# Inputs laid out in the order of their transfers, in a gated-attention kernel with a two-layer network behind it

## The chip, the cores and the metric

The kernel runs on one core of one Trainium2 chip. The metric is device time of one execution in microseconds. The core's engines are PE (TensorE, matrix products), DVE (VectorE), ACT (ScalarE), POOL (GpSimd) and SP (SyncE, which here only issues transfers); each works through its own instructions in order and waits for others by semaphores. Sixteen DMA engines carry the transfers.

## What is computed

A recurrence over 768 steps for each of 4 x 8 heads with 48 columns, and a two-layer network on its output, 3072 tokens of 384 columns with 2048 hidden ones:

```python
for t in range(S):
    state = alpha[:, :, t, :, None] * state + np.einsum('bhd,bhe->bhde', k[:, :, t], v[:, :, t])
    y[:, :, t] = np.einsum('bhd,bhde->bhe', q[:, :, t], state)
...
h = x @ w_in
beta = 1.0
neg = h <= -beta
pos = h >= beta
...
g = np.where(pos, h, np.where(neg, 0.0, (h + beta) ** 2 / (4.0 * beta)))
...
return (g @ w_out).astype(np.float32)
```

q, k, v and alpha are 32-bit floats; the two weights are 64-bit floats.

## The kernel before, in words

**Chunks.** The 3072 tokens are 24 chunks of 128; three chunks are a group. For each chunk the kernel brings alpha, k and q (`raw_a`, `raw_k`, `raw_q`) to a form with two heads of 64 rows on the partitions and tokens along the free axis. DVE runs a scan over alpha forwards and one backwards (L634, L660), multiplies k into the backward one (`inv`, L674) and q into the forward one (`Q`, L680). PE turns the keys (L701), makes scores (L716), the update of the state (L729) and the outputs (L856). V is used in two places: `vt`, with tokens on the partitions, and `both`, which holds V's rows beside the state, with the halves of the chunk swapped (its second place).

**How the inputs come.** Chunks up to `EARLY` (nine of them) come as they lie in memory, tokens on partitions, 48 columns of 4 bytes a head, which is runs of 192 bytes (L510), into two halves of one tile per input. PE turns each with four transposes (L544) into PSUM, where DVE reads them. Later chunks come by four transfers each (L528) and DVE transposes 32x32 blocks (L557) into `turn`. V's second place is copied from `vt` by ACT or POOL for the first six chunks (L594, L598), and comes by four transfers after that (L605).

**Weights.** Eight pairs of raw weights (L462, L472, L482) come as 64-bit words. ACT (L374, L382, L427), DVE (L390, L401) and POOL (L414, L429, or DVE in their place) decode each half into a high and a low 32-bit part; that is about 2 instructions on DVE, 4 on POOL and 3 on ACT for each of the sixteen halves.

**The network.** A hidden row f of a group is nine products of 128x384 (L952); then DVE and ACT apply the gate (L981, L996, L1007), ACT rounds the result to a high part (L1011), POOL subtracts it for a low part (L1012), and nine more products add into the outputs (L1030). The first `SPLIT` hidden rows of group 0 are done chunk by chunk, in products of 128x128. Groups 0 and 1 do the first half of the hidden rows each, then the second half of each, so that weights are asked for later; the other groups go one by one. Group 0 takes its last rows by way of `rest_b`; for later groups six transfers move the remainder of x into place (L901).

**What sets the order.** A planner, `Plan.order`, places every instruction with a cost in microseconds and a due time, engine by engine. Instructions may have a second engine to go to (`other`). Where it sees PE idle in the first 165 us it puts in fillers, products of zeros (L1101). Of the chunks from `MERGE` on, the outputs of one are merged with the scores of the next in one burst.

Of the kernel before, what the change touches and what calls it, by code (L numbers as in the profile page):

```python
# [8 lines left out]
F32 = mybir.dt.float32  # L9
# [19 lines left out]
EARLY = 9  # L29
# [4 lines left out]
LOAD = 6.0  # L34
# [7 lines left out]
AHEAD = 15.0  # L42
# [3 lines left out]
MERGE = 6  # L46
# [4 lines left out]
VHELP = 6  # L51
SPLIT = 1
# [25 lines left out]
class Plan:  # L78
# [7 lines left out]
    SMALL = 2.1  # L86
# [148 lines left out]
def gated_attention_ffn(ctx: ExitStack, tc: tile.TileContext, q, k, v, alpha, w_in, w_out, out):  # L235
    nc = tc.nc
    B, H, S, D = q.shape
    DM, DF = w_in.shape
    P = 128
    G = H // 2  # L240
# [31 lines left out]
    both = const.tile([P, 2, 2, G, 2, 64], F32, name="both")  # L272
# [47 lines left out]
    with ExitStack() as main:  # L320
# [7 lines left out]
        for name in ("stage", "tp", "qk", "vp", "att", "fw"):  # L328
            pool(name)
# [22 lines left out]
        wide = w_in.dtype == U64  # L352

        def decode(u, which, raw, parts, shape, key):
# [4 lines left out]
            flat = lambda t: t.rearrange(shape)  # L359
            part = lambda a: parts().rearrange(PARTS[which])[:, a * n : (a + 1) * n]  # L360
            w = raw
            data = lambda: flat(raw())
            if wide:
                w = buf("stage", "w", [P, n], 2)
                word = lambda dt, i: flat(raw()).bitcast(dt).rearrange("p (m w) -> p m w", w=2)[:, :, i]
# [47 lines left out]
                for c in cols:  # L413
                    add = lambda e, c=c: e.tensor_tensor(  # L414
                        out=bits()[:, c], in0=bits()[:, c], in1=word(I32, 0)[:, c], op=ALU.add
                    )
                    plan.op(
                        "POOL",
                        0.93,
                        key,  # L420
                        lambda add=add: add(nc.gpsimd),
                        [w, raw, (u, which)],
                        [w],
                        port=True,
                        other=("DVE", 0.9, lambda add=add: add(nc.vector), True),
                    )
            plan.op("ACT", 0.8, key, lambda: nc.scalar.copy(out=part(0), in_=data()), [w], [parts])  # L427
            for c in cols:
# [5 lines left out]
                    0.93,  # L434
# [5 lines left out]
                    other=("DVE", 0.48, lambda sub=sub: sub(nc.vector), True),  # L440
# [4 lines left out]
        def weights(u):  # L445
            fs = slice(u * NW * P, (u + 1) * NW * P)
            make = lambda shape, dt: Buf("wt", lambda: wts.tile(shape, dt, name="wt"))
            ti = make([P, KT, NW * P], w_in.dtype)
            to = make([P, NW, DM], w_out.dtype)
            key = need[u]  # L450
            pairs_of = w_in[0 : 2 * D * KT, fs].rearrange("(k r e) f -> r e k f", r=2, e=D)
            rest = w_in[2 * D * KT : DM, fs].rearrange("(r k e) f -> r e k f", r=2, k=KT)
# [3 lines left out]
            for r in range(2):  # L456
                p = 64 * r
                plan.op(
                    "SP",
                    Plan.ISSUE,  # L460
                    fetch,
                    lambda p=p, r=r: nc.sync.dma_start(out=ti()[p : p + D], in_=pairs_of[r]),  # L462
                    [],
                    [ti],
                    moved=size * 3 // 8,
                    beside=r > 0,
                )
                plan.op(
                    "SP",
                    Plan.ISSUE,  # L470
                    fetch,
                    lambda p=p, r=r: nc.sync.dma_start(out=ti()[p + D : p + 64], in_=rest[r]),  # L472
                    [],
                    [ti],
                    moved=size // 8,
                    beside=True,
                )
# [3 lines left out]
                fetch,  # L481
                lambda: nc.sync.dma_start(out=to(), in_=w_out[fs, :].rearrange("(j p) m -> p j m", p=P)),  # L482
                [],
                [to],
                moved=size,
            )
            wi[u] = make([P, 2, KT, NW, P], F32R)
            wo[u] = make([P, 2, NW, DM], F32R)
            decode(u, "i", ti, wi[u], "p k f -> p (k f)", ready)
            decode(u, "o", to, wo[u], "p j m -> p (j m)", ready + LAG)  # L490


        C = CH // 32
        flat = lambda t: t.rearrange("p g t -> p (g t)")
        pairs = lambda t: t[:, 0 : G * CH].rearrange("p (g t) -> p g t", g=G)

        def whole(t, j):

            half = t.rearrange("p g w -> p (g w)")[:, j % 2 * H * 64 : (j % 2 + 1) * H * 64]
            return half.rearrange("p (h e) -> p h e", e=64)  # L500

        def load(x, j, key):
            b, t0 = j // PER, j % PER * CH
            t, rows = raws[x], {"a": alpha, "k": k, "q": q}[x][b, :, t0 : t0 + CH, :]
            if j < EARLY:
                plan.op(
                    "SP",
                    Plan.ISSUE,
                    key,
                    lambda: nc.sync.dma_start(out=whole(t, j)[:, :, 0:D], in_=rows.rearrange("h s d -> s h d")),  # L510
                    [],
                    [(x, j % 2)],
                    moved=P * DM * 4 * Plan.SMALL,
                )
                return
            if j == EARLY:
                plan.op(
                    "POOL", 0.15, key, lambda: nc.gpsimd.memset(t[:, :, W : W + 32], 1.0), [], [(x, 0), (x, 1)]
                )
            view = rows.rearrange("(g r) (a c) d -> r a g (c d)", r=2, c=C)  # L520
            for r in range(2):
                for half in range(2):
                    p0, o = 64 * r + 32 * half, 32 * (1 - half)
                    plan.op(
                        "SP",
                        Plan.ISSUE,
                        key,
                        lambda p0=p0, o=o, r=r: nc.sync.dma_start(out=t[p0 : p0 + 32, :, o : o + W], in_=view[r]),  # L528
                        [],
                        [(x, 0), (x, 1)],  # L530
                        moved=P * DM * 2,
                        beside=r + half > 0,
                    )

        def turned(x, j, key, to=()):

            t = raws[x]
            if j < EARLY:
# [3 lines left out]
                def flip():  # L542
                    for g in range(G):
                        nc.tensor.transpose(  # L544
                            out=view()[:, g * CH : (g + 1) * CH],
                            in_=whole(t, j).rearrange("p h e -> p (h e)")[:, g * P : (g + 1) * P],
# [3 lines left out]
                flips[j] = plan.op("PE", 0.45, key, flip, [(x, j % 2)], [ps, *to], mode="full", after=[flips[j]] if j in flips else [])  # L550
                return ps, view
            o = buf("tp", "turn", [P, G * CH], 2)
            plan.op(
                "DVE",
                1.05,
                key,
                lambda: nc.vector.transpose(  # L557
                    out=pairs(o()).rearrange("p g (a c) -> p g c a", c=C),
                    in_=t[:, :, 32 : 32 + W].rearrange("p g (c d) -> p g c d", d=D)[:, :, :, 0:32],
                ),  # L560
                [(x, 0), (x, 1)],
                [o],
            )
            return o, lambda: o()
# [3 lines left out]
        def prepare(j, key):  # L568

            b, t0 = j // PER, j % PER * CH  # L570
            early = j < EARLY
            for x in "akq":
# [6 lines left out]
                lambda: nc.sync.dma_start(out=vt(), in_=v[b, :, t0 : t0 + CH, :].rearrange("h s d -> s h d")),  # L579
                [],  # L580
                [vt],
                moved=P * DM * 4 * Plan.SMALL,
            )
            for r in range(2):
                rows = slice(HC * (1 - r), HC * (2 - r))
                for u in range(2):
                    if j < VHELP:
                        to = both[rows, j % 2, u, :, r, 0:D]
                        from_ = lambda r=r, u=u: vt()[HC * u : HC * (u + 1)].rearrange("p (g r) d -> r p g d", r=2)[r]
                        plan.op(  # L590
                            "ACT",
                            0.36,
                            key + 0.2,
                            lambda to=to, from_=from_: nc.scalar.copy(out=to, in_=from_()),  # L594
                            [vt],
                            [("v", j % 2, u)],
                            beside=r > 0,
                            other=("POOL", 0.38, lambda to=to, from_=from_: nc.gpsimd.tensor_copy(out=to, in_=from_()), True),  # L598
                        )
                        continue  # L600
                    plan.op(
                        "SP",
                        Plan.ISSUE,
                        key - LOAD + 1,
                        lambda r=r, u=u, rows=rows: nc.sync.dma_start(  # L605
                            out=both[rows, j % 2, u, :, r, 0:D],
# [561 lines left out]
def stepwise(tc, q, k, v, alpha, win, wout, NF, ident, half_b, ones, out):  # L1168
# [8 lines left out]
    with ExitStack() as ctx:  # L1177
# [39 lines left out]
        with tc.For_i(0, B * S, P) as r:  # L1217
# [74 lines left out]
```

## Time and profile before

| | us |
|---|---|
| median of the runs | 534.03 |
| lowest, highest | 532.78, 534.27 |
| the profiled execution's own time | 532.99 |
| its span | 531.2 |
| busy: PE, DVE, ACT, POOL | 509.1, 378.7, 264.4, 271.7 |
| PE's wide products, hidden and output (L952, L1030) | 227.0 and 227.8 |

The span is what the profile's rows cover; the execution's own time is 1.8 us longer. Busy PE time contains the fillers. Slices are fortieths of the span, 13.28 us each. In rows of engines, "SPq" is SP's queue of transfer instructions, "PEld" is PE's loading of weights; a row of the waits reads: who waited, for whom, us in total, times, longest.

### The profile page before, as it was taken

The page shows a single profiled execution, that of the slowest core. Times are in us where ns is not written, and L with a number is a line of the kernel's source. Part 1 is how long each engine was busy: PE and PEld are TensorE (multiplying, and loading weights), DVE is VectorE, ACT ScalarE, POOL GpSimd, SP SyncE. Part 2 cuts the span into 40 slices and gives each one's busy share as a digit, 9 for nine tenths or more (in the row PEclk, how much of TensorE's full clock was granted, in tenths as well). Part 3 has the DMA queues.
Part 4 walks back from the last instruction along what each step waited for, and adds up shares of the span by engine and source line. Part 5 has one row for each costly group of instructions (what it writes and reads, how often), then busy time and mean ns, then how long its engine had stood idle before and what let it go on. Part 6 is the DMA issues. An engine that isn't in the chain of part 4 may idle for free.

```text
span 531.2 us, 12704 instructions
## 1 busy us (share of the span) xinstructions
PE 509.1 (96%) x4906; PEld 488.4 (92%) x4906; DVE 378.7 (71%) x714; ACT 264.4 (50%) x510; POOL 271.7 (51%) x332
## 2 busy tenths in 40 slices
PE   8896999798999999999999999999999999999995
PEld 6785899698899999999999999999999999999994
DVE  6998778577899796688696796688596884333331
ACT  3789897565444443444444433434434534343332
POOL 4687888699854452443452452453443452333330
PEclk9999799999999999999999999999999999999998
DMA  9999889921455634335334442345333200100001
GB/s 160 194 216 203 179 197 170 255 50 47 109 145 140 181 76 91 91 82 136 90 73 90 131 111 56 91 83 135 90 85 84 74 23 2 23 12 33 2 0 49
DMA packets 112241, 53.87 MB, mean 101 GB/s; under 512 B 77392, under 2 KB 107056, under 8 KB 112176
## 3 DMA queue, kind: packets, MB, share of 16 engines
q1 hardware_dynamic: 112176, 53.01, 44.4%
q8 instruction: 40, 0.66, 0.5%
q14 instruction: 25, 0.20, 0.1%
HBM read 45.02 MB, written 5.90 MB: 96 GB/s over the span
## 4 chain that ended last, share of the span: by engine, by line
PE 77%; DMA 5%; POOL 5%; ACT 4%; SPq 3%; DVE 3%; issue 2%; POOLq 0%; DVEq 0%; ACTq 0%
PE ps L1030 34%; PE ps L952 33%; DMA wt<-in_moe_w_in 5%; PE ps L856 4%; PE ps L729 2%; POOL wt L429 2%; PE ps L716 2%; POOL w L414 2%; PE ps L701 2%; POOL gh L1012 1%; ACT w L374 1%; SPq L510 1%; SPq L462 1%; DVE Q L634 1%; PE ps L544 1%
## 5 line engine op out<-in xcount | busy, mean ns | idle before, releaser
L1030 PE MATMUL ps<-wt,gh 128*128 128x384 f32 x1152 | 227.8, 341 | 4.4 <-POOL gh L1012 2.5
L952 PE MATMUL ps<-ring,wt 128*128 128x384 f32 (+1 forms) x1170 | 227.0, 339 | 1.9 <-DVE gf L1007 1.1
L1012 POOL TENSOR_TENSOR gh<-gf,gh 128x384 fp32r<-128x384 f32 (+1 forms) x129 | 139.7, 1084 | 166.0 <-ACT gh L1011 134.9
L952 PEld LDWEIGHTS ps<-ring,wt 128*128 128x128 f32 x1170 | 206.2, 190 | 3.8 <-DVE gf L1007 1.4
L1030 PEld LDWEIGHTS ps<-wt,gh 128*128 128x128 f32 x1152 | 200.5, 188 | 8.0 <-POOL gh L1012 4.1
L981 ACT ACTIVATE gf<-gf,half_b 128x384 f32<-128x384 f32 x122 | 74.9, 616 | 113.2 <-DVE gf L996 110.0
L1011 ACT CAST gh<-gf 128x384 fp32r<-128x384 f32 (+1 forms) x130 | 65.9, 507 | 85.9 <-DVE gf L1007 64.6
L996 DVE TENSOR_SCALAR gf<-ps 128x384 f32<-128x384 f32 x122 | 67.2, 552 | 56.5 <-PE ps L952 54.2
L1007 DVE TENSOR_TENSOR gf<-gf,ps 128x384 f32<-128x384 f32 (+1 forms) x130 | 69.8, 539 | 47.7 <-ACT gf L981 47.6
L414 POOL TENSOR_TENSOR w<-w,wt 128x384 int32<-128x384 int32 x31 | 32.7, 1070 | 10.4 <-DVE w L401 3.9
L429 POOL TENSOR_TENSOR wt<-w,wt 128x384 fp32r<-128x384 f32 x32 | 35.2, 1114 | 1.4 <-ACT wt L427 0.9
L856 PE MATMUL ps<-Q,both 128*64 128x64 f32 x372 | 27.8, 229 | 2.6 <-DVE inv L660 2.6
L856 PEld LDWEIGHTS ps<-Q,both 128*64 128x64 f32 x372 | 24.4, 141 | 5.2 <-issue 3.8
L856 PE MATMUL ps<-other,both 128*64 128x64 f32 x372 | 27.7, 229 | 0.3 <-POOL other L784 0.3
L802 DVE TENSOR_TENSOR Q<-ps,mask 64x256 f32<-64x256 f32 x48 | 20.3, 423 | 7.9 <-ACT other L766 5.2
L833 POOL TENSOR_TENSOR state<-state,last 128x192 f32<-128x192 f32 x20 | 10.1, 507 | 30.0 <-DVE state L758 29.9
L634 DVE TENSOR_TENSOR_SCAN Q<-turn,fwd 128x512 f32<-128x512 f32 x15 | 20.5, 1365 | 6.6 <-PE ps L856 6.5
L856 PEld LDWEIGHTS ps<-other,both 128*64 128x64 f32 x372 | 24.3, 141 | 0.4 <-POOL other L784 0.4
L748 ACT COPY both<-state 48x192 f32<-48x192 f32 x53 | 18.5, 349 | 7.9 <-POOL state L833 4.8
L643 POOL TENSOR_SCALAR last<-Q 128x4 f32<-128x4 f32 x24 | 5.4, 224 | 31.4 <-DVE Q L634 30.8
L680 POOL TENSOR_TENSOR Q<-Q,turn 128x512 f32<-128x512 f32 x15 | 19.5, 1299 | 3.4 <-DVE turn L557 3.4
L401 DVE SCALAR_TENSOR_TENSOR w<-wt,w 128x768 int32<-128x768 int32 x16 | 20.6, 1285 | 0.2
(92 smaller groups left out, 511.5 us busy)
## 6 DMA issues: line engine op xcount, KB each, us to landing
wt<-in_moe_w_out SPq DMA_DIRECT2D x8, 768.0 KB, 7.9
raw_a<-in_alpha SPq DMA_DIRECT2D x60, 96.0 KB, 2.2
raw_k<-in_k SPq DMA_DIRECT2D x60, 96.0 KB, 2.4
raw_q<-in_q SPq DMA_DIRECT2D x60, 96.0 KB, 2.4
vt<-in_v SPq DMA_DIRECT2D x24, 192.0 KB, 3.3
wt<-in_moe_w_in SPq DMA_DIRECT2D x16, 288.0 KB, 5.9
out<-ot SPq DMA_DIRECT2D x24, 192.0 KB, 2.9
both<-in_v SPq DMA_DIRECT2D x72, 48.0 KB, 2.5
```

The source lines that it names most:

```text
L401: lambda: nc.vector.scalar_tensor_tensor(out=bits(), in0=word(I32, 1), scalar=-0x80000000, in1=bits(), op0=ALU.bitwise_and, op1=ALU.bitwis ...
L414: add = lambda e, c=c: e.tensor_tensor(out=bits()[:, c], in0=bits()[:, c], in1=word(I32, 0)[:, c], op=ALU.add)
L429: sub = lambda e, c=c: e.tensor_tensor(out=part(1)[:, c], in0=data()[:, c], in1=part(0).bitcast(F32)[:, c], op=ALU.subtract)
L634: lambda: nc.vector.tensor_tensor_scan(flat(Q()), aT(), flat(fwd), 0.0, ALU.mult, ALU.max),
L856: nc.tensor.matmul(out=ps()[halves[r], to, halves[u]], lhsT=lhsT[:, u, r], rhs=x()[:, g, halves[u]], start=m + u == 0, stop=True, skip_gro ...
L952: nc.tensor.matmul(out=h(), lhsT=win(f, w)[:, kt], rhs=ring[:, at, kt, a, :], start=(m == 0), stop=(m == 3 * KT - 1),)
L981: lambda: nc.scalar.activation(out=gf(), in_=in_(), func=func, scale=scale, bias=bias),
L996: lambda: nc.vector.tensor_scalar(out=gf(), in0=h(), scalar1=-1.0, scalar2=1.0, op0=ALU.max, op1=ALU.min),
L1007: lambda: nc.vector.tensor_tensor(out=gf(), in0=gf(), in1=h(), op=ALU.max),
L1011: plan.op("ACT", 0.08 + 0.41 * w, key + 0.4, lambda: nc.scalar.copy(out=gh()[:, 0], in_=gf()), [gf], [gh])
L1012: sub = lambda e: e.tensor_tensor(out=gh()[:, 1], in0=gf(), in1=gh()[:, 0].bitcast(F32), op=ALU.subtract)
L1030: nc.tensor.matmul(out=o_ps[seg][t](), lhsT=gh()[:, a, (t - c0) * CH : (t - c0 + 1) * CH], rhs=wout(f, w), start=(f == f0 and i == 0), sto ...
```

## The change

The host lays every input out with numpy, without arithmetic, as one transfer will fetch it (`lay`): `tok_a`, `tok_k`, `tok_q` with tokens on the partitions and each head padded from 48 to 64 columns with its first columns again; `dim_a`, `dim_k`, `dim_q` already in the turned form, 512 tokens-by-heads wide; V for `vt` and, apart, for `both`; the weights as rows of 768 64-bit words. Each becomes one transfer of 128 partitions (two for `both`), with runs of 1.5 to 6 KB. Every chunk's raw inputs get a buffer of their own, eight in all.

Chunks 0 to 3 are still turned by PE; from the fifth on the `dim_` form is read by DVE from SBUF as it lands, so that neither PE's transposes of chunks 4 to 8 nor DVE's of later ones are there. The product of q (L592 now) has POOL as its first engine from chunk 4 on, where it had DVE up to chunk 8. V's second place comes by transfer for all chunks. The zero columns that the padding needed are no longer set by POOL. Hidden rows 0 and 1 of group 0 are split by chunk, not row 0 alone; merged bursts begin two chunks later; inputs are due 3 us ahead, not 6.

```diff
-EARLY = 9
+EARLY = 4
...
-LOAD = 6.0
+LOAD = 3.0
...
-AHEAD = 15.0
+AHEAD = 12.0
...
-MERGE = 6
+MERGE = 8
...
-SPLIT = 1
+SPLIT = 2
...
-    both = const.tile([P, 2, 2, G, 2, 64], F32, name="both")
+    both = const.tile([P, 2, 2, 2, G, 64], F32, name="both")
...
-            for r in range(2):
-                p = 64 * r
+            for x, t in (("w_in", ti), ("w_out", to)):
                 plan.op(
                     "SP",
                     Plan.ISSUE,
                     fetch,
-                    lambda p=p, r=r: nc.sync.dma_start(out=ti()[p : p + D], in_=pairs_of[r]),
+                    lambda x=x, t=t: nc.sync.dma_start(out=t(), in_=laid[x][u]),
                     [],
-                    [ti],
-                    moved=size * 3 // 8,
-                    beside=r > 0,
-                )
...
+        def load(x, j, key):
+
+            raw = raws[x, j] = buf("stage", "raw", [P, G * CH], 8)
             plan.op(
                 "SP",
                 Plan.ISSUE,
-                fetch,
-                lambda: nc.sync.dma_start(out=to(), in_=w_out[fs, :].rearrange("(j p) m -> p j m", p=P)),
+                key,
+                lambda: nc.sync.dma_start(out=raw(), in_=laid[("tok_" if j < EARLY else "dim_") + x][j]),
                 [],
...
-            o = buf("tp", "turn", [P, G * CH], 2)
-            plan.op(
-                "DVE",
-                1.05,
-                key,
-                lambda: nc.vector.transpose(
-                    out=pairs(o()).rearrange("p g (a c) -> p g c a", c=C),
-                    in_=t[:, :, 32 : 32 + W].rearrange("p g (c d) -> p g c d", d=D)[:, :, :, 0:32],
-                ),
-                [(x, 0), (x, 1)],
-                [o],
-            )
-            return o, lambda: o()
+            return raw, lambda: raw()
...
+                plan.op(
+                    "SP",
+                    Plan.ISSUE,
+                    key - LOAD + 1,
+                    lambda r=r, rows=rows: nc.sync.dma_start(
+                        out=both[rows, j % 2, r].rearrange("p u g e -> p (u g e)"), in_=laid["v_both"][j, rows]
+                    ),
+                    [],
+                    [("v", j % 2, u) for u in range(2)],
+                    moved=P * DM * 4 * 2 // 3,
+                    beside=r > 0,
+                )
...
+    e = np.arange(64) % D
+    for name, x in (("q", q), ("k", k), ("a", alpha)):
+        x = x.reshape(B, H, S // CH, CH, D)[..., e]
+        laid["tok_" + name] = x.transpose(0, 2, 3, 1, 4).reshape(NCH, CH, H * 64)
+        x = x.reshape(B, G, 2, S // CH, CH, 64)
+        laid["dim_" + name] = x.transpose(0, 3, 2, 5, 1, 4).reshape(NCH, P, G * CH)
```

Since the planner sets the order anew, three places are shown as they stand in the two programs. First SP's queue at the start of the program. Before, from the second chunk's inputs on (`raw_`, `vt`: inputs; `wt`: weights):

```order
L510 DMA raw_a<-in_alpha 128x8x48
L510 DMA raw_k<-in_k 128x8x48
L510 DMA raw_q<-in_q 128x8x48
L579 DMA vt<-in_v 128x8x48
L462 DMA wt<-in_moe_w_in 48x3x256
L472 DMA wt<-in_moe_w_in 16x3x256
L462 DMA wt<-in_moe_w_in 48x3x256
L472 DMA wt<-in_moe_w_in 16x3x256
L482 DMA wt<-in_moe_w_out 128x2x384
```

After, from the first chunk's inputs on:

```order
L470 DMA raw<-in_laid_tok_a 128x512
L470 DMA raw<-in_laid_tok_k 128x512
L470 DMA raw<-in_laid_tok_q 128x512
L507 DMA vt<-in_laid_v 128x384
L518 DMA both<-in_laid_v_both 64x512 x2
L447 DMA wt<-in_laid_w_in 128x768
L447 DMA wt<-in_laid_w_out 128x768
L470 DMA raw<-in_laid_tok_a 128x512
```

The first pair of weights has moved ahead of the second chunk's inputs, and V's second place stands ahead of both.

Second, PE at the sixth chunk (chunk 5), from the turning of its keys on. Before (L544 turns inputs, L701 keys; L952 and L1030 are the network):

```order
L544 MATMUL ps<-ident,raw_q 128x128 x4
L701 MATMUL ps<-ident,inv 128x128 x4
L952 MATMUL ps<-ring,wt 128x384 x9
L716 MATMUL ps<-Q,inv 64x64 x16
L1030 MATMUL ps<-wt,gh 128x384 x9
L729 MATMUL ps<-vt,ks 64x48 x8
L952 MATMUL ps<-ring,wt 128x384 x9
L544 MATMUL ps<-ident,raw_a 128x128 x4
L544 MATMUL ps<-ident,raw_k 128x128 x4
```

After (L613 turns keys, L864 and L942 are the network); 25 fillers and nine L942 follow:

```order
L613 MATMUL ps<-ident,inv 128x128 x4
L628 MATMUL ps<-Q,inv 64x64 x16
L942 MATMUL ps<-wt,gh 128x384 x3
L864 MATMUL ps<-ring,wt 128x384 x9
L641 MATMUL ps<-vt,ks 64x48 x8
L864 MATMUL ps<-ring,wt 128x384 x9
```

The transposes of inputs are gone; counted up to chunk 5's outputs, the network has 54 narrow and 36 wide hidden products and 27 output products in place of 27, 36 and 18. In the whole program fillers go from 90 to 128, and L544's 108 transposes become 48 (L485).

Third, POOL at the same chunk. Before (L414 and L429 decode weights, L1012 is the network's subtraction):

```order
L414 TENSOR_TENSOR w<-w,wt 128x384 x3
L784 AFFINE_SELECT other<-other 64x512
L414 TENSOR_TENSOR w<-w,wt 128x384
L643 TENSOR_SCALAR last<-Q 128x4
L429 TENSOR_TENSOR wt<-w,wt 128x384 x3
L833 TENSOR_TENSOR state<-state,last 128x192
L429 TENSOR_TENSOR wt<-w,wt 128x384
L1012 TENSOR_TENSOR gh<-gf,gh 128x384
```

After (L404 and L419 decode, L924 subtracts, L592 is the product of q):

```order
L745 TENSOR_TENSOR state<-state,last 128x192
L654 MEMSET both 48x4x48 x2
L555 TENSOR_SCALAR last<-Q 128x4
L592 TENSOR_TENSOR Q<-Q,raw 128x512
L419 TENSOR_TENSOR wt<-w,wt 128x384
L924 TENSOR_TENSOR gh<-gf,gh 128x128
L924 TENSOR_TENSOR gh<-gf,gh 128x384
L404 TENSOR_TENSOR w<-w,wt 128x384 x4
```

The product of q now stands in POOL's order among the decodes.

More of the change, by code (lines that the diff above doesn't have):

```diff
@@ L424, in decode @@
                         port=True,
-                        other=("DVE", 0.9, lambda add=add: add(nc.vector), True),
+                        other=("DVE", 0.2 + 1.4 / PIECES, lambda add=add: add(nc.vector), True),
                     )
@@ L439, in decode @@
                     port=True,
-                    other=("DVE", 0.48, lambda sub=sub: sub(nc.vector), True),
+                    other=("DVE", 0.08 + 0.8 / PIECES, lambda sub=sub: sub(nc.vector), True),
                 )
@@ L445, in weights @@
         def weights(u):
[L446 removed]
             make = lambda shape, dt: Buf("wt", lambda: wts.tile(shape, dt, name="wt"))
[L448 to L449 removed]
+            ti, to = (make(list(laid[x].shape[1:]), laid[x].dtype) for x in ("w_in", "w_out"))
             key = need[u]
[L451 to L452 removed]
             size = P * NW * DM * (8 if wide else 4)
@@ L494, in gated_attention_ffn @@
[L494 to L508, printed above, removed]
-                    key,
[L510 to L513, printed above, removed]
-                )
[L515 to L529, printed above, removed]
-                        [(x, 0), (x, 1)],
-                        moved=P * DM * 2,
-                        beside=r + half > 0,
-                    )
@@ L585, in prepare @@
                 rows = slice(HC * (1 - r), HC * (2 - r))
[L586 to L606, printed above, removed]
-                            in_=v[b, :, t0 + HC * u : t0 + HC * (u + 1), :].rearrange("(g r) s d -> r s g d", r=2)[r],
-                        ),
-                        [],
-                        [("v", j % 2, u)],
-                        moved=P * DM * Plan.SMALL,
-                        beside=r > 0,
-                    )
+                plan.op(
[10 more added lines that the diff above has]
+                )
             Q, inv = (buf("qk", x, [P, G, CH], 2) for x in ("Q", "inv"))
@@ L848, in outputs @@
             n, i = group_of[j], j % 2
-            parts = [(both[:, i, :, g], g, g) for g in range(KT if n == 0 else G)]
+            parts = [(both[:, i, :, :, g], g, g) for g in range(KT if n == 0 else G)]
             parts += [(rest_b[:, :, :, kt], KT, kt) for kt in range(KT) if n == 0]
```

118 lines of the change are left out of this document (62 added, 56 removed).

## The prediction

> **What bounds the kernel now.** I read the slices of the span first, then busy time by stretch, the chain that ended last, the waits, and the groups by shape. In the slices PE is short of work only at the front, and the wire is full until the eighth slice:
>
> ```profile
> PE   8896999798999999999999999999999999999995
> PEclk9999799999999999999999999999999999999998
> DMA  9999889921455634335334442345333200100001
> GB/s 160 194 216 203 179 197 170 255 50 47 109 145 140 181 76 91 91 82 136 90 73 90 131 111 56 91 83 135 90 85 84 74 23 2 23 12 33 2 0 49
> ```
>
> The same by stretch (busy us and instructions of PE, weight load, DVE, ACT, POOL; then clock, wire share, GB/s):
>
> ```profile
> 0.00:60.00 60.00, 50.82 (x775) 43.34 (x776) 50.56 (x101) 44.94 (x94) 42.05 (x79) 0.95 1.06 194
> 60.00:97.00 37.00, 37.00 (x342) 35.56 (x342) 27.76 (x46) 30.26 (x54) 29.41 (x32) 1.00 0.91 189
> 97.00:108.00 11.00, 7.48 (x32) 6.52 (x31) 7.54 (x14) 5.33 (x10) 8.33 (x9) 0.85 0.94 230
> 108.00:150.00 42.00, 39.29 (x392) 36.89 (x392) 32.98 (x56) 25.14 (x45) 37.76 (x39) 1.00 0.31 82
> 150.00:450.00 300.00, 299.61 (x2945) 291.89 (x2944) 232.76 (x450) 130.47 (x259) 131.83 (x155) 1.00 0.38 92
> 525.00:531.20 6.20, 0.00 (x0) 0.00 (x0) 0.00 (x0) 0.44 (x1) 0.00 (x0) 0.73 0.29 102
> ```
>
> From 150 us on PE is busy 299.61 of 300 us, so what the change takes off DVE there (a 32x32 transpose for each of three inputs of fifteen chunks) is worth nothing. The last 6.20 us are the last rows' way out and the branch, and stay. **Only the first 150 us can become shorter.** There, 0 to 60 is a stretch of DVE (50.56 us busy) with an over-full wire beside it; from 97 to 108 PE lacks 3.5 us; from 108 to 150 it lacks 2.7 with POOL at 37.76 of 42. PE's busy time at the front also holds fillers, and its clock is halved for a while:
>
> ```profile
> L1101 PE MATMUL ps<-zeros 128*128 128x256 bf16 x90 | 12.9, 297 | 1.1 <-DVE zeros L249 1.1
> 54.00:56.00 2.00, 1.90 (x32) 1.82 (x32) 1.90 (x5) 1.46 (x2) 2.00 (x3) 0.50 1.13 301
> ```
>
> **The wire.** From 2 to 8 us only the 192-byte rows of heads move; from 100 to 102 us mostly rows of weights:
>
> ```profile
> DMA packets 5863, 1.11 MB, mean 185 GB/s; under 512 B 5863, under 2 KB 5863, under 8 KB 5863
> DMA packets 372, 0.77 MB, mean 385 GB/s; under 512 B 29, under 2 KB 214, under 8 KB 372
> ```
>
> Packets of 190 B get 185 GB/s, packets of 2.1 KB get 385. After the change every input row is 1.5 to 6 KB long. An early chunk grows from 0.79 MB (four tensors) to 1.25 MB (three padded to 64 columns a head, V, and V's second place), but its wire time goes from 0.79 / 0.185 = 4.3 us to 1.25 / 0.385 = 3.2. In the new order six chunks and four weight pairs (1.57 MB each), 13.8 MB, stand up to the end of chunk 5's inputs: 36 us at 385 GB/s, 54 us at the 255 of the eighth slice. DVE starts chunk 5 at 50.80 (row below), so at 385 the wire is no limit any more and at 255 it nearly is. I take 385, as it is the row with long packets almost alone.
>
> **Where the wire shows today.** Two rows of the waits, then the chain that ended last in order of time (start, us, what):
>
> ```profile
> ACT wt L382 <- DMA wt<-in_moe_w_in: 6.3, 2, 4.0
> DVE fwd L624 <- PE ps L544: 4.0, 3, 2.5
> ```
>
> ```profile
> 50.80 0.18 DVE fwd L624
> ...
> 69.16 0.44 PE ps L544 x4
> ...
> 74.90 1.58 PE ps L952 x9
> ...
> 91.20 10.20 DMA wt<-in_moe_w_in
> ...
> 102.29 0.50 ACT gh L1011
> ...
> 102.86 1.01 POOL gh L1012
> ```
>
> ACT stands in its own order before a weight that has not landed; the rounding L1011 is behind it, POOL's L1012 behind that, and PE waits for the result. This is the hole of 97 to 108: 11 - 7.48 = 3.5 us, and 0.15 x 11 = 1.7 of lost clock, 5.2 us together.
>
> **The sum, against the profiled execution's own 532.99 us** (span 531.2; the median of the runs shown is 534.03 and their lowest 532.78, so it is an ordinary execution).
>
> 1. *DVE up to chunk 5.* Mean durations of what differs:
>
> ```profile
> L390 DVE TENSOR_SCALAR w<-w 128x768 int32<-128x768 int32 x16 | 15.4, 964 | 2.5 <-ACT w L374 2.5
> L401 DVE SCALAR_TENSOR_TENSOR w<-wt,w 128x768 int32<-128x768 int32 x16 | 20.6, 1285 | 0.2
> L414 DVE CUSTOM_DVE_ANT_0 w<-wt,w 128x768 uint16<-128x768 uint16 x1 | 0.6, 604 | 0.0
> L680 DVE TENSOR_TENSOR Q<-Q,ps 128x512 f32<-128x512 f32 x9 | 6.1, 682 | 1.1 <-PE ps L544 1.1
> L1007 DVE TENSOR_TENSOR gf<-gf,ps 128x128 f32<-128x128 f32 x3 | 0.8, 282 | 0.1
> L1007 DVE TENSOR_TENSOR gf<-gf,ps 128x384 f32<-128x384 f32 x23 | 12.4, 548 | 15.0 <-ACT gf L981 15.0
> L885 DVE TENSOR_TENSOR ring<-ps,ring 128x512 fp32r<-128x512 f32 x4 | 2.7, 684 | 1.0 <-ACT ring L880 1.0
> L758 DVE TENSOR_TENSOR state<-state,ps 128x192 f32<-128x192 f32 x14 | 4.9, 348 | 0.6 <-POOL both L751 0.4
> ```
>
> By the order, DVE does up to chunk 5's key product one each of the first four less (3.5 us) and three small activation products, one large, one split of x and one sum of the state more (0.85 + 0.55 + 0.68 + 0.35 = 2.4): -1.1. Of the 4.0 us it waited for transposed inputs, 2.5 belong to the first chunk, where the warming fillers hold PE; 1.5 can go. Against it, the first weight pair now stands ahead of chunk 1's inputs: 1.57 / 0.385 = 4.1 us of wire, which DVE fills with that pair's decode and the mask. I take **-1.5**, ends -2.6 and +2.
>
> 2. *Products done by then.* Before chunk 5's outputs the new PE order has nine groups of nine hidden or output products, the old seven: two more, so **-3.2** (1.58 each). The second split hidden row (27 narrow products in place of nine wide) and 38 more fillers lie in PE's gaps there; if they didn't, 38 x 0.143 (12.9 / 90) = 5.4 us would be the other end.
>
> 3. *Transposes that vanish.* Chunks 4 to 8 lose three times four of L544. For 4 and 5 PE has room, so nothing. Chunks 6 and 7 lie in the stretch 60 to 97, where PE is full: 6 x 0.44 = **-2.6**. Chunk 8's lie in the hole; the end is -4.0 with them.
>
> 4. *The hole at 97 to 108.* SP's new order has all but one of the sixteen weight transfers ahead of the transfer of group 1's remainder (L901 before, L813 after), where ten of the sixteen stood before; at 385 GB/s none is late. But POOL carries its decode as before, so I take back 3.5 of the 5.2: **-3.5**, ends 0 and -5.2.
>
> 5. *POOL.* It loses copies of V and gains the Q products of chunks 4 to 8, and of later chunks as before:
>
> ```profile
> L598 POOL COPY both<-vt 64x192 f32<-64x192 f32 x11 | 4.6, 420 | 0.7 <-DMA vt<-in_v 0.3
> L680 POOL TENSOR_TENSOR Q<-Q,turn 128x512 f32<-128x512 f32 x15 | 19.5, 1299 | 3.4 <-DVE turn L557 3.4
> ```
>
> That is -4.6 and -1.5 for memsets no longer there, against 5 x 1.30 = +6.5: **0**, ends -1 and +2. ACT loses the other copies; it was never last there alone.
>
> 6. *Clock.* The half clock of 54 to 60 costs 3 us; DVE's stretch still leaves PE gaps, more of them filled. **-0.6**, ends -3 and 0.
>
> Sum: -1.5 - 3.2 - 2.6 - 3.5 - 0.6 = -11.4, so **521.6 us**. The merged bursts begin two chunks later; the parts of a burst add up to what they cost singly, so nothing for that.
>
> **Rivals.**
>
> *A. POOL holds the front.* If decode and subtraction in POOL's order pace 60 to 150, terms 3 and 4 give nothing, for PE only waits elsewhere: -5.3, so 527.7. For it: 37.76 of 42. Against: before, POOL itself waited behind the late weights.
>
> *B. The front closes.* Ends of all terms, -2.6 - 3.2 - 4.0 - 5.2 - 3, and the 2.7 us of 108 to 150 too: -20.7, so 512.3. For it: POOL was idle 18 of the first 60 us, and weights that land earlier are decoded then. Against: DVE's 50.56.
>
> *C. Slower: DVE shuts POOL out.* Chunks 4 to 8 now read their inputs from SBUF where before they read PSUM. Instances of the same instructions in both places (ns least/median/most):
>
> ```profile
> L634 DVE TENSOR_TENSOR_SCAN Q<-turn,fwd x15: 1218/1227/1624, 149.1 to 422.1; 128x512 f32<-128x512 f32 x15
> L634 DVE TENSOR_TENSOR_SCAN Q<-ps,fwd x9: 1217/1224/1224, 5.7 to 136.2; 128x512 f32<-128x512 f32 x9
> L674 DVE TENSOR_TENSOR inv<-inv,turn x15: 662/687/1217, 158.2 to 433.7; 128x512 f32<-128x512 f32 x15
> L674 DVE TENSOR_TENSOR inv<-inv,ps x9: 679/687/690, 8.8 to 139.6; 128x512 f32<-128x512 f32 x9
> ```
>
> From PSUM they never stretch, from SBUF some do, by up to 0.4 and 0.5 us. Two scans and one product a chunk, 2 x 1.23 + 0.69 = 3.15 us, in five chunks are 15.8 us. If POOL stood still for all of it while being the engine that paces, the front would grow by 15.8, against the 11.4 gained: +4.4, so 537.4. It decides from the point where over 11.4 of the 15.8 us fall on POOL's busy time; the medians, unmoved in both places, speak against that. The Trainium skill, SBUF — State Buffer, section "SBUF: two separate sides", states it as a rule: a DVE instruction with two SBUF inputs and a GpSimd instruction that reads SBUF take the shared ports in turn, whole instruction by whole instruction. By that rule the whole 15.8 us would be exposed; the trace agrees that it happens (the most 1217 ns beside 687) but shows it in few instances.
>
> *D. It changes nothing.* The wire was full, but DVE's order sets the start and POOL's the rest: term 2 is eaten by the 5.4 us of fillers, and the other terms by stalls: about 533.
>
> **How the numbers follow.** Forecast 0.48, A 0.20, B 0.15, C 0.10, D 0.07. A measurement of this kernel tells a change from none at about 0.3% (1.6 us). Faster holds the forecast, A and B: 0.83; same is D, 0.07; slower is C, 0.10. Leaving out C, most of D and the lowest part of B is 2 in 10: the range goes from 513.0 to 531.0. It covers the wire at 255 GB/s too, where term 1 goes to its +2 and term 4 to nothing (528.6).
>
> **What would show it.** Term 1: chunk 5's first scan starts before 50 us. Term 2 and 3: the last of PE's half-speed slices lies earlier and PE's wide groups start sooner. Term 4: ACT's wait for weights is under 1 us and PE is full at 97 to 108. Term 5: POOL's busy time over the first 150 us stays within 2 us. The wire: slices above 300 GB/s and shares below 9 after the first 40 us. Wrong would be: a new wait of PE on L592 or L924 (POOL late), DVE waiting for chunk 1's inputs for more than 3 us, or POOL's subtraction and decode going from about 1.1 to over 1.3 us each (rival C).

## The result, and the profile after

The changed kernel is **slower**: a median of 537.34 us (536.55 to 539.07) against 532.16 (530.37 to 534.27) for the kernel before on the same chip, a ratio of 1.0095 with a 95% interval of 1.0072 to 1.0119. The forecast was 521.6 and the range ended at 531.0. The time that came out is that of rival C (537.4). An eighth execution of the changed kernel took 983.38 us, at full granted clock, and isn't counted. The profiled execution of after took 537.47 us, its span is 535.8.

The slices of after, in the same four rows as before:

```profile
PE   8889869988889999999999999999999999999996
PEclk9999998989899999999999999999999999999998
DMA  8998828221211521323211431232211110101001
GB/s 278 317 338 279 338 65 264 74 74 66 79 40 45 161 83 57 94 65 107 85 54 53 105 121 48 67 96 101 61 56 48 39 37 1 23 1 45 1 1 48
```

The wire did what was forecast: 278 to 338 GB/s in the first five slices, where it had 160 to 216, and it is far from full after the seventh. PE is short of work in the fifth and sixth slice now (54 to 80 us), where it was busy for 90% or more, and from the ninth to the twelfth (107 to 161). By stretch (busy us and instructions of PE, weight load, DVE, ACT, POOL; then clock, wire share, GB/s), after:

```profile
0.00:60.00 60.00, 52.94 (x830) 45.13 (x831) 50.42 (x99) 43.99 (x95) 42.17 (x68) 1.00 0.93 299
60.00:97.00 37.00, 31.54 (x290) 27.96 (x289) 34.99 (x48) 26.84 (x47) 32.26 (x29) 0.95 0.61 207
97.00:108.00 11.00, 9.99 (x55) 9.06 (x53) 10.76 (x17) 5.64 (x11) 9.73 (x9) 1.00 0.15 54
108.00:150.00 42.00, 37.35 (x273) 35.53 (x274) 34.98 (x51) 20.40 (x35) 40.65 (x35) 0.92 0.25 77
150.00:450.00 300.00, 298.86 (x2977) 292.16 (x2976) 202.30 (x401) 137.24 (x273) 131.12 (x151) 1.00 0.25 71
```

The hole of 97 to 108 is mostly closed (PE 9.99 of 11, it was 7.48), and its lost clock is back. But the stretch ahead of it, where PE was full, now has a hole of its own: 31.54 of 37 us. There DVE is busy 34.99 us and POOL 32.26: together they record 67 us of work in 37. From 150 us on almost nothing has changed (PE 298.86 of 300 us against 299.61).

How far PE had come is read from its wide products. The groups of before up to 60 us, then up to 150 us (instructions, busy us, mean ns; idle time ahead of them and who ended it):

```profile
L952 PE MATMUL ps<-ring,wt 128*128 128x384 f32 x25 | 6.2, 401 | 0.0
L952 PE MATMUL ps<-ring,wt 128*128 128x128 f32 x27 | 3.6, 279 | 0.5 <-POOL wt L429 0.5
L1030 PE MATMUL ps<-wt,gh 128*128 128x384 f32 x9 | 2.4, 379 | 0.0
...
L952 PE MATMUL ps<-ring,wt 128*128 128x384 f32 x213 | 43.9, 353 | 1.1 <-DVE gf L1007 1.1
L1030 PE MATMUL ps<-wt,gh 128*128 128x384 f32 x198 | 41.5, 349 | 4.4 <-POOL gh L1012 2.5 <-ACT gh L1011 2.0
```

The same of after:

```profile
L864 PE MATMUL ps<-ring,wt 128*128 128x128 f32 x54 | 7.2, 280 | 0.0
L942 PE MATMUL ps<-wt,gh 128*128 128x384 f32 x18 | 4.8, 368 | 0.5 <-POOL gh L924 0.5
L864 PE MATMUL ps<-ring,wt 128*128 128x384 f32 x23 | 4.6, 341 | 0.0
...
L942 PE MATMUL ps<-wt,gh 128*128 128x384 f32 x189 | 43.6, 367 | 7.9 <-POOL gh L924 4.2 <-POOL wt L419 1.9 <-DVE gh L924 1.6
L864 PE MATMUL ps<-ring,wt 128*128 128x384 f32 x189 | 38.2, 348 | 0.0
```

27 narrow products of a split row stand for nine wide ones. At 60 us after is ahead, 23 + 18 + 18 = 59 against 25 + 9 + 9 = 43. At 150 it is behind, 189 + 189 + 18 = 396 against 213 + 198 + 9 = 420. At 1.58 / 9 = 0.176 us each, a lead of 2.8 us has become a lag of 24 x 0.176 = 4.2 us, and the two spans differ by 4.6: the loss lies between 60 and 150 us, nearly all of it. The idle time of the output products there went from 4.4 to 7.9 us, and it is POOL's high-low subtraction (L924) and decode (L419) that end most of it.

What keeps POOL is in the timeline of after (start, duration, engine, instruction):

```profile
69.40 1.11 POOL L696 TENSOR_SCALAR_AFFINE_SELECT other<-other 64x512 f32<-64x512 f32 x1
...
69.91 3.92 DVE L924 TENSOR_TENSOR gh<-gf,gh 128x384 fp32r<-128x384 f32 x1
70.48 1.97 POOL L419 TENSOR_TENSOR wt<-w,wt 128x384 fp32r<-128x384 f32 x2
...
72.41 1.00 POOL L924 TENSOR_TENSOR gh<-gf,gh 128x384 fp32r<-128x384 f32 x1
...
83.77 1.84 DVE L546 TENSOR_TENSOR_SCAN Q<-raw,fwd 128x512 f32<-128x512 f32 x1
...
84.51 3.81 POOL L419 TENSOR_TENSOR wt<-w,wt 128x384 fp32r<-128x384 f32 x2
```

Two rows of the waits of after, up to 170 us, say the same of ACT:

```profile
ACT w L364 <- POOL wt L419: 12.2, 9, 2.7
...
ACT w L364 <- DMA wt<-in_laid_w_in: 5.2, 2, 4.8
```

At this line it still waits for weights twice, both times before 60 us; later it waits for POOL. In the timeline, at 69.91 a subtraction on DVE stands for 3.92 us while four instructions of POOL go by. At 84.51 it is the other way round: two decodes of POOL take 3.81 us beside DVE's scans of a chunk that lies in SBUF. The groups of the first 150 us, DVE's scans and POOL's three largest, after:

```profile
L546 DVE TENSOR_TENSOR_SCAN Q<-raw,fwd 128x512 f32<-128x512 f32 x6 | 10.4, 1742 | 0.2
L572 DVE TENSOR_TENSOR_SCAN inv<-raw,bwd 128x511 f32<-128x511 f32 x6 | 9.7, 1614 | 0.0
...
L572 DVE TENSOR_TENSOR_SCAN inv<-ps,bwd 128x511 f32<-128x511 f32 x4 | 5.1, 1271 | 0.0
L546 DVE TENSOR_TENSOR_SCAN Q<-ps,fwd 128x512 f32<-128x512 f32 x4 | 4.9, 1223 | 0.1
...
L419 POOL TENSOR_TENSOR wt<-w,wt 128x384 fp32r<-128x384 f32 x30 | 40.0, 1343 | 0.6 <-ACT wt L417 0.5
L404 POOL TENSOR_TENSOR w<-w,wt 128x384 int32<-128x384 int32 x26 | 30.5, 1184 | 10.8 <-ACT wt L372 4.7 <-DVE w L391 4.1 <-issue 2.0
```

A scan that reads its chunk from PSUM takes 1223 ns as ever. The same scan takes 1742 when the chunk lies in SBUF, and POOL's decode takes 1343 where it took, before:

```profile
L429 POOL TENSOR_TENSOR wt<-w,wt 128x384 fp32r<-128x384 f32 x32 | 35.2, 1114 | 1.4 <-ACT wt L427 0.9
```

### The profile page after: what moved, and what is told of

It is laid out like the page before. It is cut to its first block, busy times and chain, and to the rows that moved or that the text cites. A ratio compares the mean times of both kernels' runs of the same rounds, so it can differ in the third digit from the quotient of the medians.

```text
span 535.8 us, 12355 instructions
## 1 busy us (share of the span) xinstructions
PE 511.1 (95%) x4902; PEld 489.2 (91%) x4902; DVE 363.9 (68%) x669; ACT 264.5 (49%) x512; POOL 279.3 (52%) x312
## 2 busy tenths in 40 slices
DMA packets 27902, 52.46 MB, mean 98 GB/s; under 512 B 3808, under 2 KB 13504, under 8 KB 27840
## 4 chain that ended last, share of the span: by engine, by line
PE 72%; POOL 10%; DVE 7%; ACT 5%; issue 4%; DMA 2%; SPq 0%; POOLq 0%; DVEq 0%; ACTq 0%
PE ps L942 32%; PE ps L864 31%; POOL wt L419 4%; PE ps L768 4%; POOL gh L924 3%; POOL w L404 2%; PE ps L641 2%; PE ps L628 1%; PE ps L613 1%; DMA wt<-in_laid_w_in 1%; DVE Q L546 1%; DVE inv L572 1%; ACT gf L893 1%; ACT wt L372 1%; DVE w L380 1%
## 5 line engine op out<-in xcount | busy, mean ns | idle before, releaser
L942 PE MATMUL ps<-wt,gh 128*128 128x384 f32 x1152 | 230.9, 344 | 7.9 <-POOL gh L924 4.2
L864 PE MATMUL ps<-ring,wt 128*128 128x384 f32 (+1 forms) x1188 | 226.6, 337 | 1.1 <-DVE ring L797 1.1
L924 POOL TENSOR_TENSOR gh<-gf,gh 128x384 fp32r<-128x384 f32 (+1 forms) x129 | 141.2, 1099 | 165.5 <-ACT gh L923 118.3
L942 PEld LDWEIGHTS ps<-wt,gh 128*128 128x128 f32 x1152 | 202.6, 190 | 12.2 <-POOL gh L924 5.9
L864 PEld LDWEIGHTS ps<-ring,wt 128*128 128x128 f32 x1188 | 207.3, 189 | 2.2 <-DVE ring L797 1.3
L419 POOL TENSOR_TENSOR wt<-w,wt 128x384 fp32r<-128x384 f32 x32 | 41.9, 1322 | 0.6 <-ACT wt L417 0.5
L572 DVE TENSOR_TENSOR_SCAN inv<-raw,bwd 128x511 f32<-128x511 f32 x20 | 38.2, 1912 | 0.0
L404 POOL TENSOR_TENSOR w<-w,wt 128x384 int32<-128x384 int32 x28 | 32.5, 1173 | 10.8 <-ACT wt L372 4.7
L546 DVE TENSOR_TENSOR_SCAN Q<-raw,fwd 128x512 f32<-128x512 f32 x20 | 29.7, 1485 | 7.5 <-PE ps L768 7.2
L745 POOL TENSOR_TENSOR state<-state,last 128x192 f32<-128x192 f32 x20 | 12.1, 605 | 30.6 <-DVE state L670 30.6
L592 POOL TENSOR_TENSOR Q<-Q,raw 128x512 f32<-128x512 f32 x20 | 26.5, 1323 | 3.0 <-DVE inv L564 2.0
L616 ACT COPY ks<-ps 128x512 f32<-128x512 f32 x24 | 14.0, 584 | 24.1 <-PE ps L613 24.0
L364 ACT ACTIVATE w<-wt 128x768 f32<-128x768 f32 x16 | 14.6, 910 | 17.5 <-POOL wt L419 12.2
```

The lines of the kernel that those rows point to most:

```text
L404: add = lambda e, c=c: e.tensor_tensor(out=bits()[:, c], in0=bits()[:, c], in1=word(I32, 0)[:, c], op=ALU.add)
L419: sub = lambda e, c=c: e.tensor_tensor(out=part(1)[:, c], in0=data()[:, c], in1=part(0).bitcast(F32)[:, c], op=ALU.subtract)
L546: lambda: nc.vector.tensor_tensor_scan(flat(Q()), aT(), flat(fwd), 0.0, ALU.mult, ALU.max),
L572: lambda: nc.vector.tensor_tensor_scan(flat(inv())[:, 0:n][:, ::-1], aT()[:, 1 : n + 1][:, ::-1], flat(bwd)[:, 0:n][:, ::-1], bwd[:, G - 1 ...
L864: nc.tensor.matmul(out=h(), lhsT=win(f, w)[:, kt], rhs=ring[:, at, kt, a, :], start=(m == 0), stop=(m == 3 * KT - 1),)
L924: sub = lambda e: e.tensor_tensor(out=gh()[:, 1], in0=gf(), in1=gh()[:, 0].bitcast(F32), op=ALU.subtract)
```

## The experiments

**P** is rival C made exact: DVE, reading chunks 4 to 8 from SBUF, and POOL exclude each other. **S**: the new constants (LOAD, AHEAD, MERGE, SPLIT) give the work a worse order. **W**: the new transfers, larger in bytes, come too late. P and S were told apart first, in four kernels on one chip (before: 531.75 us, 530.34 to 532.56).

**All nine early chunks by PE and PSUM again**, in the new layout: one constant of after.

```diff
-EARLY = 4
+EARLY = 9
```

> The changed kernel with chunks 4 to 8 turned by PE again (EARLY = 9), so that DVE reads them from PSUM and the product of q is DVE's; layout, long rows and all other constants stay as changed. Theory P (DVE reading these chunks from SBUF and POOL shut each other out between 60 and 150 us): the time falls below the kernel before, 525 to 530 us, and the backward scans of chunks 4 to 8 go back to 1.27 us from 1.6. Theory S (the other constants, above all the second split row and the later due times, make the bad order): it stays at 535 to 540 us. Theory W (the transfers' longer rows and larger bytes themselves): it stays at 535 to 540 too.

Measured: 525.91 us (525.09 to 526.23), ratio 0.9887 [0.9868, 0.9906]. The loss is gone and a gain stands there.

**The old constants, chunks 4 to 8 still from SBUF:**

```diff
-LOAD = 3.0
+LOAD = 6.0
-AHEAD = 12.0
+AHEAD = 15.0
-MERGE = 8
+MERGE = 6
-SPLIT = 2
+SPLIT = 1
```

> The changed kernel with the former LOAD, AHEAD, MERGE and SPLIT, but EARLY = 4. Theory P: chunks 4 to 8 are still read from SBUF, so 535 to 540 us. Theory S: 530 us or less. Theory W: 535 to 540 us.

Measured: 535.02 us (534.14 to 535.55), ratio 1.0059 [1.0044, 1.0075]. Scans from SBUF average 1875 ns and POOL's decode 1380. The constants are worth some 2 us, not the loss.

**Both together**, `EARLY = 9` and the old constants, so that only the layout is left of the change.

> Only the layout and V's second place by transfer: EARLY = 9 and the former LOAD, AHEAD, MERGE and SPLIT. Theory P: 525 to 531 us, as the hole at 97 to 108 us closes and nothing new holds DVE. Theory S: the same. Theory W: 535 us or more.

Measured: 525.09 us (524.54 to 525.33), ratio 0.9875 [0.9856, 0.9893]. The layout by itself gains 6.7 us, and with it the new constants cost some 0.8. W falls.

**After, with ACT copying the inputs of chunks 4 to 8 into PSUM.** The transfers, the layout and the constants are those of after; DVE's operand has another place. The product of q goes to DVE with it, and the planner is told that these instructions don't shut POOL out.

```diff
+VIA = 9
...
+            if j < VIA:
+                ps = ps_a(j)
+                plan.op("ACT", 0.6, key, lambda: nc.scalar.copy(out=flat(ps()), in_=raw()), [raw], [ps, *to])
+                return ps, lambda: flat(ps())
             return raw, lambda: raw()
...
-            early = j < EARLY
+            early = j < VIA
...
-            in_ps = QHELP <= j < EARLY
+            in_ps = QHELP <= j < VIA
```

> The changed kernel, in which ACT copies the inputs of chunks 4 to 8, which come in the turned form, into PSUM, and DVE reads them there (product of q on DVE as for the chunks before); PE has no transposes of them. Theory P in its strict form (where DVE's operand lies decides): 526 to 532 us, with the backward scans of these chunks at 1.27 us. If PE's transposes or the order of the first chunks decide and not the place of the operand: 535 us or more.

Measured: 524.96 us (524.02 to 528.07), ratio 0.9863 [0.9843, 0.9882], with fifteen ACT instructions more than after. P is left; but three things went with the place (the product's engine, the planner's flag, the order). The next kernels part them.

**The exclusion by itself**: DVE instructions beside a steady queue of POOL products, in a kernel of nothing else. It computes no part of the reference.

```python
scan = lambda to, x: nc.vector.tensor_tensor_scan(to, x, fwd, 0.0, ALU.mult, ALU.max)
beside = lambda: nc.gpsimd.tensor_tensor(out=pool[:, 0:384], in0=pa, in1=pb, op=ALU.mult)
...
for dve, n in (
    (lambda: scan(scan_sb, src), 8),
    (lambda: scan(scan_ps, bank), 8),
    ...
):
    for i in range(n):
        dve()
        if i < 10:
            beside()
    meet()
```

> This kernel leaves out the whole computation: it runs DVE instructions alone, then beside a steady queue of POOL products (128x384, SBUF to SBUF), for durations only. Theory P (DVE and POOL take turns wherever DVE reads its two operands from SBUF): a scan of 128x512 that takes about 1.22 us alone takes about 2.2 us beside POOL when its input lies in SBUF (its own 1.22 and a POOL product of about 1.0 ahead of it), and POOL's products stretch likewise; with one input in PSUM it stays at 1.22 to 1.25 and POOL's at their alone time. Products of 0.68 us: about 1.7 from SBUF, 0.69 from PSUM. Theory S (only constants matter) and theory W (the wire) expect no difference between the two places: 1.22 both times.

The durations of DVE's scans (ns, least/median/most) in the order alone, from SBUF beside POOL, from PSUM beside POOL:

```profile
L41 DVE TENSOR_TENSOR_SCAN alone<-src,fwd x8: 1211/1224/1224, 4.1 to 12.9; 128x512 f32<-128x512 f32 x8
L41 DVE TENSOR_TENSOR_SCAN scan_sb<-src,fwd x8: 1212/1832/1973, 23.6 to 36.2; 128x512 f32<-128x512 f32 x8
L41 DVE TENSOR_TENSOR_SCAN scan_ps<-bank,fwd x8: 1212/1224/1224, 39.0 to 47.8; 128x512 f32<-128x512 f32 x8
```

And the groups in the stretches of POOL alone, of scans from SBUF and of scans from PSUM, in this order (busy us, mean ns):

```profile
L43 POOL TENSOR_TENSOR pool<-pa,pb 128x384 f32<-128x384 f32 x8 | 7.9, 992 | 0.6
...
L41 DVE TENSOR_TENSOR_SCAN scan_sb<-src,fwd 128x512 f32<-128x512 f32 x8 | 14.2, 1773 | 0.2
L43 POOL TENSOR_TENSOR pool<-pa,pb 128x384 f32<-128x384 f32 x8 | 13.5, 1689 | 0.5
...
L41 DVE TENSOR_TENSOR_SCAN scan_ps<-bank,fwd 128x512 f32<-128x512 f32 x8 | 9.8, 1222 | 0.2
L43 POOL TENSOR_TENSOR pool<-pa,pb 128x384 f32<-128x384 f32 x8 | 7.9, 992 | 0.5
```

POOL's product takes 992 ns alone and beside a scan from PSUM, and 1689 beside a scan from SBUF. The scan goes from 1222 to 1773 on the mean. Both are hurt, and only by the place. Products on DVE behave alike: 686 ns from PSUM, 1316 from SBUF while POOL's queue stands beside them. The price is less than expected: the eight scans start within 23.6 to 36.2 us, so a pair of scan and product goes by in 12.6 / 7 = 1.80 us and not in 1.22 + 0.99 = 2.21. The Trainium skill, SBUF — State Buffer, section "Who interferes with whom", says that a DVE instruction with at most one SBUF input doesn't contend with GpSimd outside certain faster modes; the 1222 and 992 agree. In the section "SBUF: two separate sides" it says that whichever starts first holds the shared ports for its whole instruction and that the other is fully blocked. By the measured 1.80 the two overlap for some 0.4 us of a pair, an estimate from these durations; here the measurement decides.

Then, on one chip (before: 531.98 us, 530.65 to 533.40), three kernels made from after.

**Only the product of q of chunks 4 to 8 on DVE:**

```diff
-            in_ps = QHELP <= j < EARLY
-            ways = [("DVE", 0.66, lambda: mul(nc.vector), not in_ps), ("POOL", 1.3, lambda: mul(nc.gpsimd), True)]
+            in_ps = QHELP <= j < 9
+            ways = [("DVE", 0.66, lambda: mul(nc.vector), j >= EARLY), ("POOL", 1.3, lambda: mul(nc.gpsimd), True)]
```

> After, with only the product Q of chunks 4 to 8 moved from POOL to DVE (five of 1.30 us on POOL, five of 0.69 on DVE); inputs stay in SBUF. Theory P (the scans' place in SBUF): the two scans and the inv product of each chunk still exclude POOL, and the product now does too; the time stays near after, 533 to 538, and scans from raw stay above 1.5 us on average. Theory Q (the load of five products on POOL is what made the front late, and the copies into PSUM gained by taking it off POOL): 6.5 us off POOL, 530 or less.

Measured: 538.18 us (537.19 to 538.72), ratio 1.0113 [1.0094, 1.0132]. Taking 6.5 us of instructions off POOL gives nothing, though on DVE these products read two operands from SBUF too.

**Only the planner's flag**, so that the order changes and the operands stay in SBUF:

```diff
-            vec = lambda us, emit, reads, writes, port=not early: plan.op(
+            vec = lambda us, emit, reads, writes, port=j >= 9: plan.op(
```

> After, with the planner told that the instructions of chunks 4 to 8 on DVE do not shut POOL out, while their operands still lie in SBUF: only the order changes. Theory P (the hardware's exclusion): the chip does not read the planner's flag, so the instances still stretch (scans from raw above 1.5 us) and the time is 535 to 541. Theory O (the planner's own avoidance of such pairs made the order worse, and the copies into PSUM gained by lifting it): 530 or less.

Measured: 533.39 us (530.99 to 534.33), ratio 1.0023 [1.0008, 1.0038]; the scans from SBUF still average 1805 and 1426 ns. Neither theory's interval holds it. The exclusion stays, as P says, and a part of the loss, some 4 us, was the order in which the planner stepped around it.

**ACT's copies for chunks 4 and 5 alone** (`VIA = 6`).

> After, with ACT copying the inputs of chunks 4 and 5 alone (not 6 to 8) into PSUM, and the product of these two on DVE. Theory P: each of the five chunks costs its share of the 12.4 us that lay between after (537.3) and the copies for all five (525.0), so two of five give back about 5 us: 530 to 534; scans of chunks 4 and 5 at 1.22 to 1.28, those of 6 to 8 still above 1.5. A theory by which only the start of the front matters (chunks 4 and 5 set the first group's start): all of it, 524 to 527. One by which only the stretch behind 60 us matters: nothing, 536 to 538.

Measured: 536.64 us (535.63 to 538.19), ratio 1.0091 [1.0072, 1.0109]. Two chunks of five give back 0.7 us, not 5: a miss of P's even shares, and in the range of a cost that arises behind 60 us. The last two kernels, on one chip again (before: 531.32 us, 530.48 to 532.88), test the place alone and the stretch.

**The kernel with ACT's copies, but back into SBUF.** The instructions of PE, DVE, ACT and POOL are those of that kernel, in the same order; only ACT's output and with it DVE's operand is another. (The buffer is held until DVE has read it, and SP issues one later input's transfer behind V's second place, not ahead of it.)

```diff
-                plan.op("ACT", 0.6, key, lambda: nc.scalar.copy(out=flat(ps()), in_=raw()), [raw], [ps, *to])
-                return ps, lambda: flat(ps())
+                plan.op("ACT", 0.6, key, lambda: nc.scalar.copy(out=raw(), in_=raw()), [raw], [ps, *to])
+                return ps, lambda: raw()
```

> The kernel with copies (525.0), instruction for instruction in the same order on every engine, but ACT's copies of the inputs of chunks 4 to 8 go back to their place in SBUF instead of to PSUM, so DVE reads the same five chunks from SBUF. Only the place of the operand differs. Theory P (exclusion in hardware): scans of chunks 4 to 8 above 1.5 us on average and the time back up by 7 to 10 us, 532 to 535, the rest of the 12.4 being order. Theory O (the order made by the planner, which the last run but one showed to be worth 4 us, explains it all): 526 or less.

Measured: 535.50 us (534.14 to 536.57), ratio 1.0083 [1.0066, 1.0101], against 524.96 and 0.9863 with PSUM: **10.5 us, or by the two ratios, since the chips differ, 2.2% of before (11.7 us), for the place of one operand in five chunks**. Not all of P's sizes came: the forward scans of these five chunks average 1.54 us, the backward ones 1.38, where over 1.5 was asked for. The profiled executions took 528.07 us with PSUM and 534.14 with SBUF, so their rows show 6.1 us of the difference. The stretches 60 to 97 and 97 to 108, first of the kernel with copies into PSUM:

```profile
60.00:97.00 37.00, 34.56 (x346) 32.84 (x339) 33.38 (x58) 34.34 (x64) 30.18 (x33) 1.00 0.79 257
97.00:108.00 11.00, 11.00 (x65) 11.00 (x64) 7.73 (x16) 8.99 (x16) 9.50 (x11) 1.00 0.16 48
```

and of the one with copies into SBUF:

```profile
60.00:97.00 37.00, 31.74 (x287) 29.73 (x286) 31.46 (x51) 30.41 (x57) 31.84 (x30) 1.00 0.71 232
97.00:108.00 11.00, 9.64 (x55) 9.01 (x54) 7.82 (x13) 9.36 (x16) 10.19 (x9) 1.00 0.03 10
```

In the same order, with fewer instructions done (30 against 33 on POOL, 51 against 58 on DVE), POOL is busy for longer, and PE lacks 2.8 us more in the first of the two. Over the first 150 us POOL records 112.89 us for 145 instructions with PSUM and 121.53 for 139 with SBUF, and the kernel with SBUF is then 31 wide products behind, 5.4 us at 0.176 each.

**ACT's copies for chunks 6 to 8 alone:**

```diff
+VIA = 9
+LATE = 6
...
+            if LATE <= j < VIA:
+                ps = ps_a(j)
+                plan.op("ACT", 0.6, key, lambda: nc.scalar.copy(out=flat(ps()), in_=raw()), [raw], [ps, *to])
+                return ps, lambda: flat(ps())
...
-            early = j < EARLY
+            early = j < EARLY or LATE <= j < VIA
...
-            in_ps = QHELP <= j < EARLY
+            in_ps = j < EARLY or LATE <= j < VIA
```

> After, with ACT's copies into PSUM for chunks 6 to 8 alone; 4 and 5 stay in SBUF. The copies for 4 and 5 alone gave 0.7 us. If a chunk's exclusion costs only where POOL has the last word, behind 60 us, where chunks 6 to 8 stand: 524 to 529, and chunks 4 and 5 cost nothing worth seeing. If the cost belongs to all five together (POOL's work put off in any of them has to be done later, and only without all of them is there enough room): 530 to 535.

Measured: 528.64 us (527.26 to 530.22), ratio 0.9939 [0.9922, 0.9956]. Three chunks give back 8.7 of the 12.4 us that all five give (537.34 - 524.96). Most of the cost sits where POOL has the last word. The two parts add up to 9.4 of the 12.4 us; the other 3 belong to neither alone. In both kernels the order and the product's engine changed along with the place, so these shares are rougher than the 10.5.

## Why the prediction was wrong

**The step that failed is term 5, POOL at 0**, with ends of -1 and +2, and with it the chance of 0.10 for rival C. Busy time in the first 150 us (PE, weight load, DVE, ACT, POOL) was, before:

```profile
0.00:150.00 150.00, 134.59 (x1536) 122.30 (x1537) 118.85 (x215) 105.66 (x201) 117.54 (x156) 0.97 0.80 164
```

and after:

```profile
0.00:150.00 150.00, 131.82 (x1444) 117.69 (x1445) 131.16 (x213) 96.87 (x186) 124.81 (x139) 0.97 0.61 196
```

POOL records 7.3 us more for 17 instructions fewer, where the prediction's sign was within 2, and DVE 12.3 more for 2 fewer. The term counted POOL's own instructions and let their durations stand; what it left out cost 12.4 us by the runs. Of the signs for rival C one came (decode at 1343 ns, over 1.3 us) and one did not (the wide subtraction at 1184 ns, 1164 before). The products that were moved onto POOL are not what hurts most: back on DVE, they leave the time where it was (538.18). What hurts is an instruction of DVE that was in the program before and only reads from elsewhere.

**Why C was rated low.** The argument was that the medians from SBUF, 1227 and 687 ns, were as short as those from PSUM. But the instances from SBUF began at 149.1 and 158.2 us, and the row of 150 to 450 that the prediction quotes has POOL busy for 131.83 of 300 us there, 44%. The chunks that the change moves, 4 to 8, begin at 39, 51, 66, 100 and 136 us in before, where POOL is busy for 42.05 of 60 us, 29.41 of 37, 8.33 of 11 and 37.76 of 42: 70 to 90%. The rows were true, and of another stage. The planner also steps around such pairs where there is room (its flag `port`), which keeps a median calm. Rows of the right stage were at hand in the trace of before. DVE's L401 reads two operands from SBUF; its instances (ns, least/median/most) were:

```profile
L401 DVE SCALAR_TENSOR_TENSOR w<-wt,w x16: 948/980/2856, 17.9 to 141.3; 128x768 int32<-128x768 int32 x16
```

The longest is 1.9 us over the median, and the mean of 1285 that the prediction quotes is 0.3 us over it.

**Rival C had the mechanism; that its time was met is luck.** It set a price of 15.8 us against a gain of 11.4. The runs give a price of 12.4 (after against the copies into PSUM) and a gain of 7.3 (that kernel against before, 0.0137 x 532.16). Both are measured from the same kernel, so their difference, +5.1, must agree with the +5.2 of the result and tests nothing. What tests C are the two sizes: too large by 3.4 and 4.1 us, which cancel. POOL did not stand still for all of DVE's time, as C had it; both engines stretch and partly overlap. Of the 12.4, the place is worth 10.5 (11.7 by the ratios) when the order is held, and an order that ignores it 4.0 when the place is held; the two overlap and don't add.

**The other terms.** The wire moved 299 GB/s over the first 60 us, where it moved 194, and no longer keeps anything back behind 60, as said. *Term 1*: wrong as measured. Chunk 5's first scan begins at 51.33 us, where 51.14 was before and under 50 was asked for. With chunks 4 to 8 in PSUM through PE (`EARLY = 9`) it begins at 48.73, so the term was there in that order. Between 39 and 50 us five instructions of DVE take 6.20 us in after and 3.90 there, which is most of the lag of 2.6. But with the order held the scan begins at 52.46 from PSUM and 50.63 from SBUF, so that the stretching alone ate the term isn't shown. *Term 2* held: 16 products more by 60 us, 2.8 us against 3.2. *Term 3*, the transposes of chunks 6 and 7, doesn't show: the stretch in which they vanished lost 5.5 us of PE. Its size alone isn't settled; the kernel that keeps these transposes (525.91) and the one that has ACT's copies in their place (524.96) differ by 1 us. *Term 4* held in its own stretch: by the two rows of 97 to 108 PE does 55 instructions there, all wide products, and did 32; 23 x 0.176 = 4.0 us against 3.5. Its signs were not met: ACT still waits 5.2 us for weights, early on, and PE lacks 1.0 of the 11 us. And part of it comes back ahead of the stretch, as rival A said: with `EARLY = 9` PE is full from 97 to 108, but busy for only 35.10 of the 37 us before, which were full. *Term 6*: the mean clock of the first 150 us is 0.97 in both, so nothing. Together the terms gave 7 us where the exclusion is away, not 11.4; the 1.9 us that PE lacks from 60 to 97 with `EARLY = 9` may be part of the rest, and where the remainder belongs stays open.

A better kernel than both is among the runs: the layout with PE's transposes (525.09 with the old constants), or with ACT's copies into PSUM (524.96).

## What to carry to other kernels

Before an operand of a DVE instruction is moved from PSUM to SBUF, look at what POOL does in the same stretch: where DVE reads two operands from SBUF and POOL reads SBUF too, each engine stretched the other here (1.22 and 0.99 us alone, 1.80 a pair together), so the busy times of both have to fit into the stretch nearly one after the other. Take the durations that argue for or against such contention from the stage into which the work moves, not from a calmer one. A copy by an engine with room (15 of 0.6 us on ACT here) can cost less than the contention that it removes.

## What the runs showed of the hardware that was not expected

The engine that is kept out doesn't always get the next turn. The subtraction on DVE at 69.91 us stood for 3.92 us, behind the remainder of one instruction of POOL and three whole ones, with no wait of its own in the trace; the shortest instance of the same instruction in that trace is 559 ns. A kernel of nothing but the pair shows a milder form: a scan and a product every 1.80 us, and each stretched by 0.55 to 0.70 us.
